# Start addresses modulo 512 bytes of TensorE's operands, and row maxima that begin one step later, in a gated attention and MLP kernel

## The chip, the cores and the metric

The kernel runs on one core of one Trainium2 chip. The metric is the device time of one execution in microseconds (us), as a median of several runs. A second number is the span of a profiled execution: the time from its first to its last recorded instruction, a little less than that execution's device time.

## The reference

The input x has 2048 tokens of 448 numbers. A gate, an attention block with 16 heads of 28, and an MLP behind a layer norm are computed from the same x and mixed.

```python
qkv = (x @ wqkv).reshape(B, S, 3, H, Dh)          # 16 heads of 28
scores = einsum("bhqd,bhkd->bhqk", q, k) * Dh**-0.5
a = (softmax(scores) @ v) @ wo
h = gelu(layernorm(x) @ w1 + b1)                  # 448 -> 1792
b = h @ w2 + b2                                   # 1792 -> 448
g = sigmoid((x * gate_w).sum(-1, keepdims=True))
out = g * a + (1 - g) * b
```

Everything is float32.

## The kernel before

**Precision.** Nearly every matrix is split in two, a high part in TensorE's rounded fp32 form and the low rest. A product a·b becomes three matmuls in a row: high·high, high·low, low·high. In the code the parts carry an h or an l at the end of their names (`w2h`, `w2l`, `hh`, `hl`, `qh`, `ql`, `khi`, `klo`, `woh`, `wol`, `oh`, `ol`).

**The two operands of a matmul.** A matmul first loads a block of 128 columns of one matrix into the array (the weight load, PEld in the profile). This text calls it the fixed matrix. Then the rows of the other matrix stream through it, up to 512 columns; this is the moving matrix. `mlp2` keeps 128 columns of `hh` or `hl` fixed and moves a 448-column row of `w2h` or `w2l` (1792 bytes in each partition, that is 3.5 times 512). The output projection keeps a piece of the attention's result fixed and moves `woh` or `wol`, 448 columns too. In the attention's scores a 128-token piece of the keys is fixed and 512 query columns of `qh` or `ql` move.

**Stages, in order of time.**

1. Up to 113.6 us: q, k and v. Lines L220 and L322 are the q and k products (512 columns), L232 the v product (450 columns, of `wvh` and `wvl`). ScalarE rounds, VectorE and GpSimd subtract, SyncE's queue moves data. `v_tile` sends v from three buffers `vt0` to `vt2` in turn (L236).
2. 113.6 to about 467 us: the MLP, in four chunks c of 512 tokens. `mlp1(c, f)` (L613) makes one of 14 column blocks f in 11 matmuls into PSUM bank f % 2; ScalarE applies gelu twice (L616 into `hh[f]`, L617 into a buffer `h`), GpSimd subtracts (L618 into `hl[f]`). `mlp2(c, i)` (L626, L627, L631) makes one of 16 tiles of 128 tokens in 14 x 3 matmuls. In chunk 0 the weights w1 and w2 are also fetched and split (`high_w1`, `low_w1`, `high_w2`, `low_w2`) between the products.
3. 467 us to the end: attention, in steps of five units (later seven). A unit is one head of a group of four with 128 keys and 512 queries: three products (L563) and an exponential on ScalarE (L567); the four heads' units of one piece of keys then go into the sum over values (L830). The output projection (L735 to L737) runs for each query chunk of the last group.

**Row maxima.** The softmax needs the maximum of each query row before the attention. `RowMax.issue` computes extra score products for it (L440), in groups of six during the MLP: four heads sit in different quarters of the array, so four of them run at the same time, then two more. VectorE reduces each pair (L422). `Filler.spread` sets an even rate between a first step and a limit of 482 such products by the end of the MLP; `Filler.run` is called behind the matmuls and issues a group when it is due. In chunk 0 the spread starts at f == `FS`. The keys for it, `khr`, are loaded by GpSimd's queue at f == 1 (L503, four transfers, one for each quarter), behind the subtraction L618 of f = 0.

**Order.** Instructions of each engine are written in program order and executed in that order. Tile pools are stacks of addresses; a pool that opens takes addresses of a closed one, and the first writer of a tile waits for the last users of whatever lay there. In stage 2 `hh` and `hl` lie where `wh`, `wl`, the staging buffers of q and k, `vt0` to `vt2` and the layer norm's small tiles were.

**Addresses modulo 512 bytes, before.** Counted from the built program: the three moving rows of an mlp2 block start at 0, 256, 0 for f up to 10 and at 0, 0, 0 for f above 10, where a row of 448 columns ends 256 further on than it starts. `hh` and `hl` start at 320 (f up to 6), 256 (7 to 10) and 0 (above 10). The projection moves rows that start at 0 or 256, the high and the low one of a head group at the same offset, and keeps matrices fixed at 256 (384 for the last group, each of whose pieces starts 512 further on). `wvh` and `wvl` start at 0, with `xh` and `xl` fixed at 0. `qh`, `ql` and all keys start at 0. Matrices of 512 columns are 2048 bytes long, so a row of them ends at the offset at which it starts.

Of the kernel before, what the change touches and what calls it, by code (L numbers as in the profile page):

```python
# [7 lines left out]
F32 = mybir.dt.float32  # L8
F32R = mybir.dt.float32r
# [6 lines left out]
P = 128  # L16
S = 2048
D = 448
# [4 lines left out]
CH = 512  # L23
# [7 lines left out]
MLP_MAX = 482  # L31
MLP_G = MLP_MAX // 260
MG = 6
FS = 4
WARM = 10
W1, W2 = 0.233, 0.205
SHIFTS = {10: 64, 6: 16}
LQ = 12
STEPS = (2, 5, 7, 8, 9, 10)
LSTEPS = (1, 3, 5, 6, 7, 8)  # L40
# [3 lines left out]
def kernel(ctx: ExitStack, tc: tile.TileContext, xt, wqk, wv, wo, xk, w1, b1, w2, b2,  # L44
# [38 lines left out]
    w1h, w1l, w2h, w2l = {}, {}, {}, {}  # L83
# [73 lines left out]
    with tc.tile_pool(name="qx", bufs=2) as qx, tc.tile_pool(name="qo", bufs=4) as qo, \  # L157
# [24 lines left out]
            nc.scalar.activation(wh[:, m], wt[m], AF.Copy)  # L182
            nc.gpsimd.tensor_sub(wl[:, m], wt[m], wh[:, m].bitcast(F32))

        wvh, wvl = (qw.tile([P, 4, CH], F32R, name=f"wv{x}")[:, :, :450] for x in "hl")
        vt = [qw.tile([P, H, 32], F32, name=f"vt{i}") for i in range(3)]

        xh, xl = {}, {}
# [112 lines left out]
        for what, i in turns:  # L301
# [18 lines left out]
            for k, m, t in ops:  # L320
                w, x = wl if k == "lh" else wh, xl[0] if k == "hl" else xh[0]
# [48 lines left out]
        for n in range(NM, 11 * NC):  # L370
            for what, a in ahead[n]:
                what(*a)
            c, m = divmod(n, 11)
# [124 lines left out]
    def load_khr(g, k=None, queue=nc.sync):  # L498

        sl = slice(0, S) if k is None else slice(k * CH, (k + 1) * CH)  # L500
        for j in range(4):
            r = D + (4 * g + j) * DH
            queue.dma_start(khr[32 * j:32 * j + DH, sl].bitcast(F32), qk[0, r:r + DH, sl])  # L503
# [27 lines left out]
    qs = {}  # L531

    def load_q(n):

        g, c = divmod(n, NC)
        qs[n] = aq.tile([P, CH], F32R, name="qh", bufs=3), aq.tile([P, CH], F32R, name="ql", bufs=3)
        for i in range(2):
            for j in range(4):
                r = (4 * g + j) * DH
                nc.sync.dma_start(qs[n][i][32 * j:32 * j + DH].bitcast(F32), qk[i, r:r + DH, c * CH:(c + 1) * CH])  # L540
# [52 lines left out]
    mw2 = ml.enter_context(tc.tile_pool(name="mw2", bufs=1, reuse_waits="tile"))  # L593
    mh = ml.enter_context(tc.tile_pool(name="mh", bufs=1, reuse_waits="tile"))
    for f in range(NF):
        w2h[f], w2l[f] = (mw2.tile([P, CH if f > 10 else D], F32R, name=f"w2{x}{f}")[:, :D] for x in "hl")
    hh, hl = {}, {}
    more = [mh.tile([P, CH], F32, name=f"more{i}") for i in range(2)]
    for f in reversed(range(NF)):
        if f in SHIFTS:  # L600
            mh.tile([P, SHIFTS[f]], F32, name=f"shift{f}")
        hh[f] = mh.tile([P, CH], F32R, name=f"hh{f}")
        hl[f] = mh.tile([P, CH], F32R, name=f"hl{f}")

    def mlp1(c, f):

        ps = bank[:, f % 2]
        ops = []
        for t in range(3):
            ops += [(w1h[f][:, t], yh[:, t]), (w1h[f][:, t], yl[:, t]), (w1l[f][:, t], yh[:, t])]  # L610
        ops += [(w1h[f][:, 3], yh[:, 3]), (w1l[f][:, 3], yh[:, 3])]
        for i, (a, b) in enumerate(ops):
            nc.tensor.matmul(ps, a, b, start=(i == 0), stop=(i == len(ops) - 1))  # L613
            filler.run(W1 if c else 0.65 * W1)
        h = mh.tile([P, CH], F32, name="h", bufs=2)
        nc.scalar.activation(hh[f], ps, AF.Gelu_apprx_tanh, bias=b1s[:, f:f + 1])  # L616
        nc.scalar.activation(h, ps, AF.Gelu_apprx_tanh, bias=b1s[:, f:f + 1])  # L617
        nc.gpsimd.tensor_sub(hl[f], h, hh[f].bitcast(F32))  # L618
# [21 lines left out]
    with texts:  # L640
# [12 lines left out]
        for c in range(NC):  # L653
            for f in range(NF):
                if c == 0:
# [9 lines left out]
                    if f == 1:  # L665
                        load_khr(0, queue=nc.gpsimd)
                    if f == FS:
                        filler.spread(nc.sync, MLP_MAX, 11 * W1 * (0.65 * (NF - FS) + 3 * NF) + W2 * (3 * NF * (NT - 1) - 24))
                mlp1(c, f)
# [7 lines left out]
            if c == NC - 1:  # L677
                m0.close()
                aq = ctx.enter_context(tc.tile_pool(name="aq", bufs=1, side="right", reuse_waits="tile"))

                first = {3: aq.tile([P, S], F32, name="klo", bufs=2), 2: aq.tile([P, NT, P], F32, name="vg", bufs=2)}

                def early(n, p):
                    t = first[n] if n == 3 else first[n].rearrange("p a b -> p (a b)")
                    return t[:, :n * CH].rearrange("p (n c) -> p n c", c=CH)

                nc.scalar.activation(gate, zall, AF.Exp, scale=-1.0)
                load_khi(0)
                load_klo(0)
                load_q(0)  # L690
                load_v(0)
                load_qm(0)
            else:
                ln_load(c + 1)
                ln_fetch(c + 1, 0)
                ln_fetch(c + 1, 1)
# [15 lines left out]
    def sb(name, bufs, side="left"):  # L712
        return ctx.enter_context(tc.tile_pool(name=name, bufs=bufs, reuse_waits="tile", side=side))

    ap = sb("ap", 4)
    aw = sb("aw", 1)
    ao = sb("ao", 2)
    woh = aw.tile([P, NG, D], F32R, name="woh")
    wol = aw.tile([P, NG, D], F32R, name="wol")

    b2b = aw.tile([P, D], F32, name="b2b")
    sel = aw.tile([P, P], F32, name="sel")

    outcome = [[aw.tile([P, S], F32R, name=f"o{x}{g}") for x in "hl"] for g in range(NG - 1)]
    acc = {}

    def project(c, i, oh, ol, po, groups):

        sl = slice(i * P, (i + 1) * P)
        for g in groups:  # L730
            if g < NG - 1:
                h, l = (x[:, c * CH:(c + 1) * CH][:, sl] for x in outcome[g])
            else:
                h, l = oh[:, sl], ol[:, sl]
            nc.tensor.matmul(po, h, woh[:, g], start=(g == 0), stop=False)  # L735
            nc.tensor.matmul(po, h, wol[:, g], start=False, stop=False)  # L736
            nc.tensor.matmul(po, l, woh[:, g], start=False, stop=(g == NG - 1))  # L737

    def gated(c, i, po):
        tt = c * TPC + i  # L740
        a = acc[c][:, i]
        nc.vector.scalar_tensor_tensor(a, po, gate[:, tt:tt + 1], a, op0=OP.mult, op1=OP.add)
        nc.sync.dma_start(out[tt], a)

    def finish(g, c, pv):

        ob = ao.tile([P, CH], F32, name="ob")
        rc = ao.tile([P, CH], F32, name="rc")
        lt = ao.tile([P, CH // 32], F32, name="lt")
        nc.vector.tensor_copy(ob, pv)  # L750
        nc.gpsimd.dma_start(lt, ob[DH:P:32, :])  # L751
        yield True
        nc.vector.reciprocal(lt, lt)
        r = rls[g * NC + c]
        nc.gpsimd.dma_start(r.rearrange("j (a b) -> (j a) b", b=CH // 32), lt)
        for j in range(4):
            nc.gpsimd.dma_start(rc[32 * j:32 * j + 32], r[j].partition_broadcast(32))
        yield True
        if g < NG - 1:
            oh, ol = (x[:, c * CH:(c + 1) * CH] for x in outcome[g])  # L760
        else:
            oh, ol = ao.tile([P, CH], F32R, name="oh", bufs=1), ao.tile([P, CH], F32R, name="ol", bufs=1)
        nc.gpsimd.tensor_mul(ob, ob, rc)
        nc.gpsimd.tensor_copy(oh, ob)
        nc.gpsimd.tensor_sub(ol, ob, oh.bitcast(F32))
        if g < NG - 1:
            return
        yield True
        for i in range(TPC):
            po = bank[:, 6, :D]  # L770
            project(c, i, oh, ol, po, range(NG))
            gated(c, i, po)
            yield True
# [61 lines left out]
    with tc.manual_schedule(engines=ENGINES):  # L835
# [7 lines left out]
        while u < 4 * steps:  # L843
# [4 lines left out]
            while at < units[-1] // 4:  # L848
                at += 1
                n, k = divmod(at, NT)  # L850
                g, c = divmod(n, NC)
# [18 lines left out]
                if k == 2 and n + 1 < NG * NC:  # L870
                    load_q(n + 1)
# [28 lines left out]
            if ended:  # L900
                n = summed // NT - 1
                fin, since, when = finish(n // NC, n % NC, pv), 0, LSTEPS if late else STEPS
                next(fin)
            elif fin is not None and since in when:
                next(fin, None)
# [58 lines left out]
```

## Time and profile before

| | |
|---|---|
| median of 3 runs | 1114.77 us (1114.1 to 1116.31) |
| profiled execution: its own time | 1114.39 us |
| profiled execution: span | 1112.6 us |
| TensorE matmul busy | 1104.5 us (99% of the span) |
| TensorE weight load busy | 675.4 us (61%) |
| VectorE busy | 741.3 us (67%) |
| ScalarE busy | 634.7 us (57%) |
| GpSimd busy | 334.2 us (30%) |

The clock that TensorE was granted is 1.0 throughout. Matmuls overlap in the record: the duration of one is longer than the distance to the next one's start, and the busy share of TensorE cannot show whether it runs at its peak. What one matmul costs is therefore read from starts: the time from the start of the first of a stretch to the start behind the last, divided by their number. A line such as "113.63 14.94 PE L613 MATMUL ... x65" of the timeline gives the start, the time from there to the end of the last, engine, line and count; "[0.66 <-issue]" behind it is idle time before it and what ended it.

### The profile page before, as it was taken

How to read it: one execution, taken by the hardware profiler on the slowest of the kernel's cores; microseconds unless marked ns; L12 is line 12 of the kernel's file. 1: busy time of each engine (PE TensorE's matmuls, PEld its weight loads, DVE VectorE, ACT ScalarE, POOL GpSimd, SP SyncE). 2: the span in 40 equal slices, each digit the busy share in tenths (PEclk: the TensorE clock that was granted, in tenths of full speed). 3: DMA queues.
4: the chain of work that ended last, by engine and by line, in shares of the span. 5: the costliest groups of instructions: out<-in, count | busy, mean ns of one | idle time of the engine just before them, and what ended most of it. 6: DMA issues, size and time to landing. Idle time of an engine off the chain costs nothing.

```text
span 1112.6 us, 19807 instructions
## 1 busy us (share of the span) xinstructions
PE 1104.5 (99%) x8156; PEld 675.4 (61%) x8156; DVE 741.3 (67%) x1030; ACT 634.7 (57%) x660; POOL 334.2 (30%) x354
## 2 busy tenths in 40 slices
PE   9999999999999999999999999999999999999998
PEld 7888777777777767744444444444444444454545
DVE  4553488988988889576676766667667667746103
ACT  5334640331240232287887887877878878847572
POOL 5025664343334331013112221320223024342350
PEclk9999999999999999999999999999999999999999
DMA  7988641011121022162100220012011003002111
GB/s 266 356 275 272 177 123 44 9 47 46 41 56 37 25 63 77 52 159 77 28 20 19 61 75 18 20 28 53 29 56 37 18 20 94 12 26 70 51 36 59
DMA packets 53079, 84.35 MB, mean 76 GB/s; under 512 B 8516, under 2 KB 28500, under 8 KB 52076
## 3 DMA queue, kind: packets, MB, share of 16 engines
q1 hardware_dynamic: 48732, 76.27, 22.0%
q0 software_dynamic: 4256, 6.81, 2.5%
q8 instruction: 64, 1.05, 0.4%
q14 instruction: 27, 0.22, 0.1%
HBM read 56.40 MB, written 26.49 MB: 75 GB/s over the span
## 4 chain that ended last, share of the span: by engine, by line
PE 98%; DVE 1%; ACT 1%; DMA 1%; issue 0%; SPq 0%; ACTq 0%
PE bank L830 22%; PE bank L563 20%; PE bank L440 16%; PE bank L613 13%; PE bank L220 5%; PE bank L631 5%; PE bank L626 4%; PE bank L627 4%; PE bank L232 3%; PE bank L322 1%; PE bank L735 1%; PE bank L736 1%; PE bank L737 1%; DMA raw<-in_xt 1%; ACT khi L567 0%
## 5 line engine op out<-in xcount | busy, mean ns | idle before, releaser
L567 ACT ACTIVATE pt<-bank 128x1536 f32<-128x1536 f32 (+1 forms) x386 | 460.1, 1242 | 121.8 <-PE bank L563 121.8
L420 DVE TENSOR_REDUCE mx<-bank 128x1 f32<-128x512 f32 x618 | 409.6, 687 | 174.3 <-PE bank L440 160.1
L830 PE MATMUL bank<-pt,vg 128*32 128x512 f32 x1942 | 260.4, 602 | 0.0
L422 DVE TENSOR_REDUCE mx<-bank 128x2 f32<-128x1024 f32 x203 | 238.8, 1219 | 29.9 <-PE bank L440 29.6
L440 PE MATMUL bank<-khi,qd 28*128 28x512 f32 x512 | 241.8, 480 | 0.1
L440 PEld LDWEIGHTS bank<-khi,qd 28*128 28x128 f32 x512 | 92.6, 182 | 148.1 <-DVE mx L420 106.0
L563 PE MATMUL bank<-qh,klo 28*128 28x512 f32 x1024 | 174.3, 394 | 0.0
L563 PE MATMUL bank<-qh,khi 29*128 29x512 f32 x768 | 156.5, 481 | 0.8 <-ACT khi L567 0.6
L613 PE MATMUL bank<-y,w1f 128*128 128x512 f32 x616 | 151.9, 398 | 0.0
L613 PEld LDWEIGHTS bank<-y,w1f 128*128 128x128 f32 x616 | 112.7, 188 | 33.1 <-issue 10.9
L563 PE MATMUL bank<-ql,khi 28*128 28x512 f32 x768 | 129.1, 390 | 0.0
L618 POOL TENSOR_TENSOR hl<-h,hh 128x512 fp32r<-128x512 f32 x56 | 72.9, 1301 | 117.6 <-ACT h L617 77.5
L616 ACT ACTIVATE hh<-bank,b1s 128x512 fp32r<-128x512 f32 x56 | 38.6, 689 | 99.0 <-PE bank L613 97.5
L830 PEld LDWEIGHTS bank<-pt,vg 128*32 128x32 f32 x1942 | 44.7, 108 | 78.5 <-issue 78.0
L563 PEld LDWEIGHTS bank<-qh,klo 28*128 28x128 f32 x1024 | 87.5, 185 | 3.5
L637 ACT ACTIVATE h<-bank 128x448 f32<-128x448 f32 x16 | 8.7, 546 | 137.5 <-PE bank L631 103.3
L751 POOL DMA_DIRECT2D lt<-ob x15 | 10.9, 725 | 252.6 <-DVE ob L750 252.6
L631 PE MATMUL bank<-w2h,hl 128*128 128x448 f32 x224 | 84.9, 379 | 0.0
L563 PEld LDWEIGHTS bank<-qh,khi 29*128 29x128 f32 x768 | 60.7, 182 | 39.6 <-ACT pt L567 24.9
L626 PE MATMUL bank<-w2h,hh 128*128 128x448 f32 x224 | 83.2, 371 | 0.0
L627 PE MATMUL bank<-w2l,hh 128*128 128x448 f32 x224 | 81.8, 365 | 0.0
L440 PE MATMUL bank<-khr,qd 28*128 28x512 f32 x512 | 80.4, 467 | 0.9 <-issue 0.7
(135 smaller groups left out, 1296.5 us busy)
## 6 DMA issues: line engine op xcount, KB each, us to landing
qk<-hl SPq DMA_DIRECT2D x28, 512.0 KB
raw<-in_xt SPq DMA_DIRECT2D x16, 256.0 KB
vs<-vt SPq DMA_DIRECT2D x16, 256.0 KB
s<-in_xt SPq DMA_DIRECT2D x16, 256.0 KB
rc<-rls POOLq DMA_DIRECT2D x60, 64.0 KB, 2.2
w1f<-in_xk SPq DMA_DIRECT2D x8, 448.0 KB
gbs<-h SPq DMA_DIRECT2D x16, 224.0 KB
klo<-qk SPq DMA_DIRECT2D x16, 224.0 KB
```

The source lines that it names most:

```text
L220: nc.tensor.matmul(ps, a, b, start=(i == 0), stop=(i == len(ops) - 1))
L420: nc.vector.reduce_max(self.mx[:, c0:c0 + 1], bank[:, b0], axis=AX)
L422: nc.vector.reduce_max(self.mx[:, c0:c1 + 1:c1 - c0], bank[:, b0:b1 + 1], axis=AX)
L440: nc.tensor.matmul(bank[:, b], self.qds[self.n][r, i * P:(i + 1) * P], khi[self.n // NC][r, k * 512:(k + 1) * 512], start=True, stop=True)
L563: nc.tensor.matmul(bank[:, p], a[r, k * P:(k + 1) * P], b[r], start=(i == 0), stop=(i == 2))
L567: nc.scalar.activation(t, bank[:, at[0]:at[-1] + 1], AF.Exp, scale=SCALE)
L613: nc.tensor.matmul(ps, a, b, start=(i == 0), stop=(i == len(ops) - 1))
L618: nc.gpsimd.tensor_sub(hl[f], h, hh[f].bitcast(F32))
L626: nc.tensor.matmul(a, hh[f][:, sl], w2h[f], start=(f == 0), stop=False)
L627: nc.tensor.matmul(a, hh[f][:, sl], w2l[f], start=False, stop=False)
L631: nc.tensor.matmul(a, hl[f][:, sl], w2h[f], start=False, stop=(f == NF - 1))
L830: nc.tensor.matmul(pv[32 * j:32 * j + 32, :], vg[n // NC][:, k, 32 * j:32 * j + 32], probs.pop(4 * step + j), start=(k == 0), stop=(k == N ...
```

## The change

The weights of the second MLP product are packed without gaps, and for odd f the low part lies in front of the high part, so that the moving rows of one f start at 0, 256, 0 and those of the next at 256, 0, 256: each starts where the last one ended, modulo 512. `hh` and `hl` all start at 64. `wol` moves 256 bytes on, so that a high and a low row follow each other in the same way; the attention's results start at 64 (320 for the last group). `wvh` and `wvl` start at 192 (their rows still don't begin where the last ended: 450 columns are 1800 bytes). `qh` starts at 64, with `ql` and the keys at 0 as before. The row maxima's spread starts at f = 5 instead of 4, with the same limit of 482 products.

```diff
-FS = 4
+FS = 5
-SHIFTS = {10: 64, 6: 16}
+LINE = 16
...
-        wvh, wvl = (qw.tile([P, 4, CH], F32R, name=f"wv{x}")[:, :, :450] for x in "hl")
+        wvh, wvl = (qw.tile([P, 4, CH], F32R, name=f"wv{x}")[:, :, 3 * LINE:3 * LINE + 450] for x in "hl")
...
-        qs[n] = aq.tile([P, CH], F32R, name="qh", bufs=3), aq.tile([P, CH], F32R, name="ql", bufs=3)
+        qs[n] = (aq.tile([P, CH + P], F32R, name="qh", bufs=3)[:, LINE:LINE + CH],
+                 aq.tile([P, CH], F32R, name="ql", bufs=3))
...
-        w2h[f], w2l[f] = (mw2.tile([P, CH if f > 10 else D], F32R, name=f"w2{x}{f}")[:, :D] for x in "hl")
+        t = {x: mw2.tile([P, D], F32R, name=f"w2{x}{f}") for x in ("lh" if f % 2 else "hl")}
+        w2h[f], w2l[f] = t["h"], t["l"]
     hh, hl = {}, {}
     more = [mh.tile([P, CH], F32, name=f"more{i}") for i in range(2)]
+    mh.tile([P, LINE], F32, name="shift")
     for f in reversed(range(NF)):
-        if f in SHIFTS:
-            mh.tile([P, SHIFTS[f]], F32, name=f"shift{f}")
         hh[f] = mh.tile([P, CH], F32R, name=f"hh{f}")
         hl[f] = mh.tile([P, CH], F32R, name=f"hl{f}")
...
     woh = aw.tile([P, NG, D], F32R, name="woh")
+    aw.tile([P, 4 * LINE], F32, name="gap")
     wol = aw.tile([P, NG, D], F32R, name="wol")
...
+    aw.tile([P, LINE], F32, name="shift")
     outcome = [[aw.tile([P, S], F32R, name=f"o{x}{g}") for x in "hl"] for g in range(NG - 1)]
...
+        if not (g or c):
+            ao.tile([P, 2 * LINE], F32, name="gap", bufs=1)
```

What else this does to the program, read from the built order of instructions: the number of instructions is the same on every engine, and in the attention their order is the same too. The row maxima still come in 81 groups; the first stands one f later (behind the tenth product of f = 6 instead of f = 5), four instead of five fall into chunk 0's `mlp1`, and the last groups stand where they stood. Since `hh` and `hl` lie 1792 bytes lower, some waits move. ScalarE's table load ahead of the first gelu waited for a VectorE result and the layer norm's DMAs; now a wait for the products of f = 0, and for the DMA of `vt2`, stands ahead of it. The wait for the DMA of the last `vt0` moves from f = 2 to f = 1. On SyncE the second load of the row maxima's queries (four transfers) goes behind two weight loads instead of ahead of them.

## The prediction

> **What bounds the kernel.** I read the page first: busy shares, granted clock, and the chain that ended last.
>
> ```profile
> PE 1104.5 (99%) x8156; PEld 675.4 (61%) x8156; DVE 741.3 (67%) x1030; ACT 634.7 (57%) x660; POOL 334.2 (30%) x354
> ...
> PEclk9999999999999999999999999999999999999999
> ...
> PE 98%; DVE 1%; ACT 1%; DMA 1%; issue 0%; SPq 0%; ACTq 0%
> PE bank L830 22%; PE bank L563 20%; PE bank L440 16%; PE bank L613 13%; PE bank L220 5%; PE bank L631 5%; PE bank L626 4%; PE bank L627 4%; PE bank L232 3%; PE bank L322 1%; PE bank L735 1%; PE bank L736 1%; PE bank L737 1%; DMA raw<-in_xt 1%; ACT khi L567 0%
> ```
>
> TensorE is on the path for 98% of the span, at full clock. So a nanosecond saved on a matmul is a nanosecond saved, and the change is about nothing but such nanoseconds. Its parts touch mlp2 (13% of the chain), the projection and v (3% each), the scores (20%). The busy time can't price them; starts can. The chain in order of time has long stretches of one line:
>
> ```profile
> 25.02 8.95 PE bank L232 x44
> 33.96 17.49 PE bank L220 x77
> 87.07 12.52 PE bank L220 x55
> 99.81 5.04 PE bank L220 x22
> ```
>
> L220 moves 512 columns, each row starting where the last ended: 17.49/77 = 227.1 ns, 12.52/55 = 227.6, 5.04/22 = 229.1. L232 moves 450 columns and jumps by 248 bytes at each start: 8.95/44 = 203.4. Then mlp2, in stretches of the timeline with no row maxima between (first and last start of twelve products each, at f = 0 to 4, 9 to 13, and 8 to 12):
>
> ```profile
> 175.29 0.37 PE L626 MATMUL bank<-w2h,hh 128*128 128x448 f32 x1
> ...
> 177.71 0.37 PE L626 MATMUL bank<-w2h,hh 128*128 128x448 f32 x1
> ...
> 250.02 0.36 PE L626 MATMUL bank<-w2h,hh 128*128 128x448 f32 x1
> ...
> 252.45 0.36 PE L626 MATMUL bank<-w2h,hh 128*128 128x448 f32 x1
> ...
> 159.62 0.36 PE L626 MATMUL bank<-w2h,hh 128*128 128x448 f32 x1
> ...
> 162.10 0.37 PE L626 MATMUL bank<-w2h,hh 128*128 128x448 f32 x1
> ```
>
> That is 605, 607.5 and 620 ns for a block of three products, or 201.7, 202.5 and 206.7 each. The first stretch jumps once in three starts; the second mixes both layouts; the third does too, and is the dearest I found. So something other than the column count does cost up to 5 ns, but the layout alone doesn't decide it.
>
> **The second MLP product.** There are 16 x 14 = 224 blocks of three. With no jumps the nearest row is L220's 227.1 ns, less 64 columns. A column costs at most 227.1/512 = 0.444 ns and, by the difference of L220 and L232, at least (227.1 - 203.4)/62 = 0.382. So 448 columns would take 198.7 to 202.7 ns; I take the middle, 200.7, or 602 a block. Against 606, between the two common stretches, that is -4 ns x 224 = -0.90 us. Ends: 198.7 (596 a block) gives -2.2 us; the other end is no gain, and 206.7 everywhere would give +3.1 us.
>
> **The projection.** Its 192 products run at
>
> ```profile
> 1077.11 0.36 PE L735 MATMUL bank<-woh,oh 128*128 128x448 f32 x1
> ...
> 1078.73 0.36 PE L737 MATMUL bank<-woh,ol 128*128 128x448 f32 x1
> ```
>
> 1.62/8 = 202.5 ns. Going to 200.7 gives -0.35 us; ends 198.7 and 206.7, -0.7 and +0.8 us.
>
> **The v product.** 176 products keep their jump; only the distance to the fixed matrix changes. I take nothing; the ends are 227.1 x 450/512 = 199.6 (-0.7 us) and 206.7 (+0.6 us).
>
> **Row maxima one step later.** The first group stalls today, the second doesn't:
>
> ```profile
> 113.63 14.94 PE L613 MATMUL bank<-y,w1f 128*128 128x512 f32 x65
> 128.50 0.50 PE L440 MATMUL bank<-khr,qd 28*128 28x512 f32 x3
> 129.66 0.51 PE L440 MATMUL bank<-khr,qd 28*128 28x512 f32 x3 [0.66 <-issue]
> 130.09 4.83 PE L613 MATMUL bank<-y,w1f 128*128 128x512 f32 x20
> 134.85 0.73 PE L440 MATMUL bank<-khr,qd 28*128 28x512 f32 x6
> 135.51 0.73 PE L613 MATMUL bank<-y,w1f 128*128 128x512 f32 x2
> ```
>
> 130.09 - 128.50 = 1.59 us against 135.51 - 134.85 = 0.66: the fourth quarter's product comes 0.93 us late. What it waits for is its quarter of the keys, sent by GpSimd's queue:
>
> ```profile
> 117.71 1.29 POOL L618 TENSOR_TENSOR hl<-h,hh 128x512 fp32r<-128x512 f32 x1 [5.87 <-ACT h L617]
> 118.94 2.27 POOL L503 DMA_DIRECT2D khr<-qk x4
> ...
> DMA to landing us min/median/max: 6.9/7.6/8.9
> ```
>
> The last of the four is issued at about 120.7 and 8.9 later it is 129.6, where the product starts. One step is 11 x 14.87/65 = 2.52 us, so a start at 131.0 finds the keys there: -0.93 us. The group count is the same, so no group's cost is added.
>
> **The table load.** It is the one wait that the lower addresses put in a bad place:
>
> ```profile
> 114.45 1.28 ACT L616 ACT_TABLE_LOAD   x1
> 116.37 0.69 ACT L616 ACTIVATE hh<-bank,b1s 128x512 fp32r<-128x512 f32 x1 [0.64 <-PE bank L613]
> 116.95 0.68 ACT L617 ACTIVATE h<-bank,b1s 128x512 f32<-128x512 f32 x1
> 118.91 0.69 ACT L616 ACTIVATE hh<-bank,b1s 128x512 fp32r<-128x512 f32 x1 [1.27 <-issue]
> ```
>
> Today it fits in the 1.9 us before the products of f = 0 are done at 116.37. Behind that wait it pushes both gelus by 1.28 us: the second ends at 118.91 instead of 117.63. Queued behind it on ScalarE is f = 1's gelu, which starts at 118.91 anyway. TensorE waits for it too: f = 2 reuses the bank of f = 0 and starts at 113.63 + 22 x 0.2288 = 118.66. That is 0.25 us late, with the hand-over 0.3: +0.30 us (ends 0 and 0.6). GpSimd waits as well: its subtraction ends 1.28 later, and behind it stand the four transfers of the keys. They would land at 130.9, and the first group comes at 131.0 + 0.3 = 131.3. The cover is 0.4 us; without it the stall is back in part, at most by the 0.93 that I booked. SyncE's moved loads of the next queries have the time of some seven groups of row maxima; they cost nothing.
>
> **The scores.** One step of the attention:
>
> ```profile
> 708.84 0.50 PE L440 MATMUL bank<-khi,qd 28*128 28x512 f32 x1
> 708.85 0.51 PE L563 MATMUL bank<-qh,khr 29*128 29x512 f32 x3
> 709.19 0.40 PE L563 MATMUL bank<-qh,klo 28*128 28x512 f32 x3
> 709.42 0.39 PE L563 MATMUL bank<-ql,khr 28*128 28x512 f32 x3
> 709.55 0.50 PE L563 MATMUL bank<-qh,khr 29*128 29x512 f32 x2
> 709.66 0.39 PE L440 MATMUL bank<-khi,qd 28*128 28x512 f32 x1
> 709.89 0.40 PE L563 MATMUL bank<-qh,klo 28*128 28x512 f32 x2
> 710.12 0.49 PE L440 MATMUL bank<-khi,qd 28*128 28x512 f32 x1
> 710.54 1.07 PE L830 MATMUL bank<-pt,vg 128*32 128x512 f32 x8
> 711.54 0.50 PE L440 MATMUL bank<-khi,qd 28*128 28x512 f32 x1
> ```
>
> It takes 2.70 us, some 200 times (1024 units, five at a time, later seven). Today everything in it starts at 0, so nothing jumps. With qh alone at 64 the moving row jumps when qh follows something else or is followed by it: about six times a step, 1200 in all. For that the keys lie 64 bytes from qh, and three rounds a step follow each other at 0.23 us, so that their pace is the stream's and not a weight load's. Neither price is in the trace, since nothing jumps by 64. The spread in mlp2 bounds both: (620 - 605)/3 = 5 ns. So the jumps cost at most 1200 x 5 = +6.0 us, the distance gives at most 3 x 200 x 5 = -3.0 us. The common stretches differ by only 2.5 ns in a block, less than 1 ns a product, which is the nearer row, and at such prices the two cancel: I take nothing.
>
> **The sum.** -0.90 - 0.35 - 0.93 + 0.30 = -1.88 us on the profiled execution's 1114.39, which is 0.4 below the median: 1112.5 us. A measurement of this kernel can tell about 0.2% from no change, 2.2 us; against the median the forecast lies at that bound.
>
> **The rivals.**
>
> *Addresses cost TensorE nothing.* The 605 and 607.5 of two quite different layouts speak for it, the 620 against. Then only the two stalls count: 1114.39 - 0.63 = 1113.8 us. Two pages of the Trainium skill say as much: "SBUF — State Buffer", section "SBUF: two separate sides", gives TensorE ports of its own on which it waits for nobody, and "TensorE: Matmul & The Clock Gate", section "Back-to-back issue gap", gives a distance of the columns at 2.4 GHz plus 2.5 ns, with no term for an address. By that rule 512 and 448 columns take 215.8 and 189.2 ns; the trace has 227.1 and 201.7, so it does not agree in size, and something that the rule lacks is in these 11 to 12 ns.
>
> *The distance pays in the scores.* The three rounds a step gain the full 5 ns while jumps by 64 cost little: 1112.5 - 3.0 = 1109.5 us. For it speaks that the stage is the longest and that keys and queries now start at one offset; against it that L220 does so too and runs no slower for its length than mlp2.
>
> *The jumps of qh make it slower.* Each of 1200 new jumps costs the 5 ns of the worst stretch: 1112.5 + 6.0 = 1118.5 us. It decides from 4.5/1200 = 3.8 ns a jump, where 1117.0 is passed. For it speaks that L232, which jumps at every start, takes 203.4 where L220's pace would give 199.6; against it that several jumps fall on rounds which wait for a weight load (709.19 after 708.85 is 0.34, not 0.23).
>
> **Chances.** Forecast 0.38, the scores pay 0.26, addresses cost nothing 0.16, slower by jumps 0.20. Some 0.24 of the forecast's case lies beyond the bound, and nearly all of the second: faster 0.49. The rest of the forecast, the third case and a little of the fourth: same 0.32; slower 0.19. The range leaves out about a tenth at each end, the full prices of the two cases in the scores: 1109.3 to 1116.8 us; the forecast's own is 1111.0 to 1114.0.
>
> **What would show it.** In the timeline: no idle time before the fourth product of the first group of row maxima; the table load at 116.4 and the products of f = 2 some 0.3 us late; blocks of mlp2 at 602 ns at every f, the projection near 201 ns, v still at 203. In the attention, the distance of two steps: 2.70 us if I am right, 2.685 if the distance pays, 2.73 if the jumps do harm. Mlp2 blocks that stay at 606 would refute the main term, steps off by over 10 ns the zero for the scores.

## The result: 0.3% slower, and where the time went

The changed kernel takes 1118.41 us (median of 7 runs, 1117.95 to 1119.56); the kernel before, run beside it, 1114.16 us (1113.36 to 1116.31). The ratio is 1.0032, with a 95% interval of 1.0021 to 1.0043. The forecast was 1112.5 us, in a range of 1109.3 to 1116.8: wrong in sign, and the time lies outside the range. The profiled execution of the changed kernel took 1119.22 us, with a span of 1117.4 against 1112.6 before.

The page of the changed kernel, its busy line and its chain that ended last (shares of the span by engine, then by line):

```profile
PE 1108.0 (99%) x8156; PEld 677.4 (61%) x8156; DVE 749.9 (67%) x1030; ACT 634.5 (57%) x660; POOL 333.7 (30%) x354
...
PE 94%; DVE 3%; issue 1%; ACT 1%; DMA 0%; SPq 0%; DVEq 0%; ACTq 0%
PE bank L836 22%; PE bank L564 20%; PE bank L440 15%; PE bank L615 11%; PE bank L220 5%; PE bank L633 4%; PE bank L628 4%; PE bank L629 4%; PE bank L232 3%; DVE mx L422 2%; PE bank L322 1%; PE bank L739 1%; PE bank L740 1%; PE bank L741 1%;
```

VectorE now holds 3% of the chain, 2% with the reductions of the row maxima (L422). Before, it held 1% and no single line of it was listed. The stages say where. Each goes from the first start of one line's products in the timeline to the first start of the next one's; the attention is taken from its first product behind the last one of mlp2, because five of its units already stand inside mlp2's last tile:

| stage | before, us | after, us | difference |
|---|---|---|---|
| up to the first product of mlp1 | 113.63 | 113.94 | +0.31 |
| mlp1, chunk 0 | 40.27 | 38.99 | -1.28 |
| **mlp2, chunk 0** | **43.04** | **49.56** | **+6.52** |
| mlp1 and mlp2, chunks 1 to 3 | 270.47 | 270.41 | -0.06 |
| attention up to the first product of the projection | 512.94 | 512.44 | -0.50 |
| the rest, to the end of the span | 132.26 | 132.07 | -0.19 |

The sum is +4.8, the difference of the spans. Nearly all the loss lies in one stage, in which no weight was added, and of products only one group of six row maxima. In the timeline of the changed kernel (start, time from there to the end of the last, engine, line, count, idle time before and what ended it), the first tile of that stage reads:

```profile
155.86 0.73 PE L440 MATMUL bank<-khr,qd 28*128 28x512 f32 x6
...
159.46 0.37 PE L629 MATMUL bank<-w2l,hh 128*128 128x448 f32 x1
160.51 0.50 PE L440 MATMUL bank<-khr,qd 28*128 28x512 f32 x2 [0.69 <-DVE mx L422]
161.64 0.50 PE L440 MATMUL bank<-khr,qd 28*128 28x512 f32 x2 [0.63 <-DVE mx L422]
162.77 0.79 PE L440 MATMUL bank<-khr,qd 28*128 28x512 f32 x2 [0.63 <-DVE mx L422]
163.50 0.74 PE L633 MATMUL bank<-w2h,hl 128*128 128x448 f32 x1
164.03 0.57 PE L628 MATMUL bank<-w2h,hh 128*128 128x448 f32 x1
...
168.89 0.57 PE L629 MATMUL bank<-w2l,hh 128*128 128x448 f32 x1
...
170.36 0.37 PE L628 MATMUL bank<-w2h,hh 128*128 128x448 f32 x1
...
172.79 0.37 PE L628 MATMUL bank<-w2h,hh 128*128 128x448 f32 x1
```

A group of six row-maxima products goes through in one piece at 155.86. The next one comes out two by two, each pair waiting for a reduction: from 159.46 to 163.50, 4.0 us, where such a step takes about 1.0 (L629 to L633 with a group between them). After it thirteen distances of mlp2's products take 168.89 - 164.03 = 4.86 us, 374 ns each; from 170.36 to 172.79 twelve take 2.43, 202.5 ns each. The windows view of the same stretch (length, then busy time and count of PE, PEld, DVE, ACT and POOL, then the granted clock of TensorE, the DMA engines' share and GB/s):

```profile
159.00:161.00 2.00, 1.31 (x7) 0.60 (x5) 2.00 (x3) 0.00 (x0) 0.00 (x0) 1.00 0.81 185
161.00:163.00 2.00, 0.74 (x6) 0.41 (x4) 2.00 (x3) 0.00 (x0) 0.33 (x1) 0.90 0.63 219
163.00:165.00 2.00, 2.00 (x6) 1.43 (x7) 2.00 (x3) 0.00 (x0) 1.92 (x2) 0.50 0.00 0
```

VectorE is busy without a break, TensorE for 1.31 and 0.74 of 2 us, and from about 162.6 to 169.4 us TensorE was granted half its clock. So the stage pays three times: some 3 us of waiting, some 2.7 us of products at half clock, and 0.8 us for one group that the later start moved into this stage from mlp1 of chunk 0 (which is why mlp1 became shorter by more than its stall).

Why VectorE was behind stands 35 us earlier, in chunk 0 of mlp1. Rows of the timeline of the changed kernel (engines ACT, DVE, POOL):

```profile
116.69 1.28 ACT L618 ACT_TABLE_LOAD   x1 [1.95 <-PE bank L615]
...
126.42 7.01 DVE L118 TENSOR_TENSOR w2l<-lnr,w2h 128x448 fp32r<-128x448 f32 x1 [3.38 <-ACT w2h L115]
...
159.25 6.87 DVE L422 TENSOR_REDUCE mx<-bank 128x2 f32<-128x1024 f32 x6
...
126.68 1.29 POOL L620 TENSOR_TENSOR hl<-h,hh 128x512 fp32r<-128x512 f32 x1
127.93 1.28 POOL L108 TENSOR_TENSOR w1f<-s,w1f 128x512 fp32r<-128x512 f32 x1
...
131.68 1.27 POOL L620 TENSOR_TENSOR hl<-h,hh 128x512 fp32r<-128x512 f32 x1
```

And of the kernel before:

```profile
125.61 1.55 DVE L118 TENSOR_TENSOR w2l<-lnr,w2h 128x448 fp32r<-128x448 f32 x1 [2.59 <-ACT w2h L115]
...
125.38 1.30 POOL L618 TENSOR_TENSOR hl<-h,hh 128x512 fp32r<-128x512 f32 x1
126.63 1.69 POOL L108 TENSOR_TENSOR w1f<-s,w1f 128x512 fp32r<-128x512 f32 x1
```

The same subtraction of w2's low part takes 7.01 us instead of 1.55. Before, VectorE gets in behind the GpSimd operation that runs when it is issued (125.38 + 1.30), and GpSimd's next one waits for it (1.69 instead of 1.28). After, GpSimd is 1.6 us later (its subtraction of f = 0 starts at 119.32 instead of 117.71; 1.3 us of that is the table load, the rest the later start of mlp1). VectorE's subtraction is issued at 126.42. Five GpSimd operations, the first at 126.68 and the last at 131.68, follow each other without a gap to 132.95, and VectorE's ends only behind the last of them, at 133.43. The Trainium skill, page "SBUF — State Buffer", section "SBUF: two separate sides", says that a VectorE operation with two inputs in SBUF and a GpSimd operation that reads SBUF need the same pair of ports, which one of them holds for the whole of its instruction. The trace agrees with that. By the same section of the Trainium skill, whichever starts first gets the pair; it leaves open who is next when both have work waiting. Here VectorE lost five times in a row.

From then on VectorE runs behind. The subtractions of the last weights end at 159.3, which is 6.4 us into mlp2; with the same start of the row maxima and the early table load (a kernel below) they end 3.5 us into it. Only then come six reductions, of the group of 155.86 and of the next, one behind the other (6.87 us). TensorE waits for them.

### The profile page after: what moved, and what is told of

Same layout as the page of the kernel before. It is cut to its first block, busy times and chain, and to the rows that moved or that the text cites. A ratio compares the mean times of both kernels' runs of the same rounds, so it can differ in the third digit from the quotient of the medians.

```text
span 1117.4 us, 19808 instructions
## 1 busy us (share of the span) xinstructions
PE 1108.0 (99%) x8156; PEld 677.4 (61%) x8156; DVE 749.9 (67%) x1030; ACT 634.5 (57%) x660; POOL 333.7 (30%) x354
## 4 chain that ended last, share of the span: by engine, by line
PE 94%; DVE 3%; issue 1%; ACT 1%; DMA 0%; SPq 0%; DVEq 0%; ACTq 0%
PE bank L836 22%; PE bank L564 20%; PE bank L440 15%; PE bank L615 11%; PE bank L220 5%; PE bank L633 4%; PE bank L628 4%; PE bank L629 4%; PE bank L232 3%; DVE mx L422 2%; PE bank L322 1%; PE bank L739 1%; PE bank L740 1%; PE bank L741 1%; DVE w2l L118 1%
## 5 line engine op out<-in xcount | busy, mean ns | idle before, releaser
L422 DVE TENSOR_REDUCE mx<-bank 128x2 f32<-128x1024 f32 x203 | 238.8, 1219 | 27.9 <-PE bank L440 27.5
L440 PE MATMUL bank<-khi,qd 28*128 28x512 f32 x512 | 241.7, 479 | 0.1
L440 PEld LDWEIGHTS bank<-khi,qd 28*128 28x128 f32 x512 | 92.4, 181 | 148.4 <-DVE mx L420 105.3
L633 PE MATMUL bank<-w2h,hl 128*128 128x448 f32 x224 | 86.1, 384 | 0.0
L440 PE MATMUL bank<-khr,qd 28*128 28x512 f32 x512 | 81.2, 468 | 2.1 <-DVE mx L422 2.1
L629 PE MATMUL bank<-w2l,hh 128*128 128x448 f32 x224 | 82.6, 369 | 0.0
```

Source lines behind the costliest of these rows:

```text
L422: nc.vector.reduce_max(self.mx[:, c0:c1 + 1:c1 - c0], bank[:, b0:b1 + 1], axis=AX)
L440: nc.tensor.matmul(bank[:, b], self.qds[self.n][r, i * P:(i + 1) * P], khi[self.n // NC][r, k * 512:(k + 1) * 512], start=True, stop=True)
L629: nc.tensor.matmul(a, hh[f][:, sl], w2l[f], start=False, stop=False)
L633: nc.tensor.matmul(a, hl[f][:, sl], w2h[f], start=False, stop=(f == NF - 1))
```

## The experiments

Three theories were set against each other. T1: the later start of the row maxima does it alone. T2: the table load, which now waits for the products of f = 0, puts GpSimd late; VectorE's subtraction is locked out, VectorE falls behind, and the groups that the later start puts into the first tile of mlp2 run into it. T3: the new addresses do it (the jumps of `qh`). T2 stands here in the form that it took after the first run; before that run it said that VectorE's lateness alone would do it, whatever the start. Stage lengths below are taken as in the table above.

### Changed kernel, row maxima from f = 4 again

```diff
-FS = 5
+FS = 4
```

> The changed kernel with the row maxima starting at f = 4 again; all its addresses stay. Theory 1 (the late start alone: it puts two groups of row maxima into the first tile of mlp2 while VectorE still splits w2): no group waits for VectorE in that tile, the clock stays at 1.0, and what is left is the addresses: 1114.5 us, between 1113.5 and 1115.5. Theory 2 (the displaced wait before the table load lets GpSimd run without a gap, VectorE's subtraction for f = 1 takes 7 us instead of 1.6, and VectorE never catches up): that subtraction still takes about 7 us and a group still waits by more than 1 us: 1117 to 1118.5 us. Theory 3 (the jumps of qh and the other addresses cost it): 1118 us, with the attention longer than before; the attention's span in the changed kernel, 0.7 us shorter than before, speaks against it already.

Measured: 1115.34 us, ratio to the kernel before 1.0002 (0.9991 to 1.0014). The loss is gone, though the new addresses and the late table load (117.24 us) are there. But VectorE's subtraction is still locked out:

```profile
126.94 5.79 DVE L118 TENSOR_TENSOR w2l<-lnr,w2h 128x448 fp32r<-128x448 f32 x1 [3.33 <-ACT w2h L115]
...
158.69 1.58 DVE L118 TENSOR_TENSOR w2l<-s,w2h 128x448 fp32r<-128x448 f32 x1
160.72 3.49 DVE L422 TENSOR_REDUCE mx<-bank 128x2 f32<-128x1024 f32 x3 [0.46 <-PE bank L440]
...
153.08 0.73 PE L440 MATMUL bank<-khr,qd 28*128 28x512 f32 x6
160.19 0.73 PE L440 MATMUL bank<-khr,qd 28*128 28x512 f32 x6
```

With this start no group falls between 153.08 and 160.19, and VectorE has caught up by then. So T3, which had 1118 us for this kernel, is out. T2 as it was first written, 1117 to 1118.5 us, failed too, and the time was that of T1: the late VectorE alone makes no group wait in mlp2. It isn't free: mlp1 of chunk 0 takes 40.94 us here and 40.11 with the early table load (a run below), mainly because TensorE waits for the late gelu at f = 2, and the second and third group for VectorE (their steps take 0.84 and 1.09 us, and 0.69 and 0.66 there).

### Kernel before, row maxima from f = 5

```diff
-FS = 4
+FS = 5
```

> The kernel before with the row maxima starting at f = 5; no address changes. Theory 1: the group at f = 9 of the first tile of mlp2 waits for VectorE for 2 to 3 us, the clock falls to 0.5 for about 7 us, and the time is 1117.5 to 1119 us. Theory 2: VectorE's subtraction for f = 1 takes under 2 us, no group waits for more than 0.5 us, the clock stays at 1.0, and the time is that of before less the first group's stall of 0.93 us: 1113.2 us. Theory 3: 1113.2 us as well.

Measured: 1113.84 us, ratio 0.9990 (0.9980 to 0.9999). Mlp1 of chunk 0 takes 38.48 us instead of 40.27, mlp2 43.83 instead of 43.04 (the moved group). T1 is out: the later start alone is a small gain.

### Changed kernel, early table load

1536 bytes more under the hidden tiles put them off the buffer `vt2` that made the table load wait; modulo 512 every address stays.

```diff
-    mh.tile([P, LINE], F32, name="shift")
+    mh.tile([P, LINE + 384], F32, name="shift")
```

> The changed kernel with 1536 bytes more ahead of hh and hl, three times 512, so that every address is the same modulo 512 but hh of f = 0 no longer lies on vt2: the table load stands ahead of the wait for the products again, as before the change. Row maxima still start at f = 5. Theory 1: the stall and the half clock stay; only the table load's 0.3 us goes: 1118 us. Theory 2: the subtraction for f = 1 takes under 2 us, the group at f = 9 waits by less than 0.5 us, the clock stays at 1.0: 1112.5 to 1113.5 us. Theory 3: 1118 us without stall.

Measured: 1113.43 us, ratio 0.9986 (0.9977 to 0.9996). In its timeline the load is early, the subtraction short, and the groups of the first tile go through:

```profile
115.45 1.28 ACT L618 ACT_TABLE_LOAD   x1
...
126.59 1.54 DVE L118 TENSOR_TENSOR w2l<-lnr,w2h 128x448 fp32r<-128x448 f32 x1 [2.58 <-ACT w2h L115]
...
156.06 0.73 PE L440 MATMUL bank<-khr,qd 28*128 28x512 f32 x6
159.96 0.73 PE L440 MATMUL bank<-khr,qd 28*128 28x512 f32 x6
```

### Early table load, row maxima from f = 4

```diff
-FS = 5
+FS = 4
...
-    mh.tile([P, LINE], F32, name="shift")
+    mh.tile([P, LINE + 384], F32, name="shift")
```

> The fourth corner: the table load early (the hidden tiles three times 512 bytes higher, as in the kernel with the wider shift), row maxima from f = 4, all other addresses as in the changed kernel. T2 (the loss needs both the late table load and the later start): 1114.0 to 1115.0 us, no half clock, VectorE's subtraction of f = 1 at 1.5 us, the first group's stall of before back. T1 (the later start alone): as the kernel of before, 1114.2. T3 (addresses): 1116 or more.

Measured: 1114.31 us, ratio 0.9996 (0.9987 to 1.0006), the subtraction at 1.54 us, mlp1 of chunk 0 at 40.11. That fills the square:

| | row maxima from f = 4 | from f = 5 |
|---|---|---|
| table load early | 0.9996 (new addresses); 1 (before) | 0.9986 (new addresses); 0.9990 (before's) |
| table load late | 1.0002 (new addresses) | **1.0032** (the change); 1.0048 (before's, the next run) |

### Kernel before, made to wait

Every address of the kernel before modulo 512, row maxima from f = 5, and one staging tile moved from below the hidden tiles to above, so that `hh0` comes to lie on `vt2`.

```diff
-FS = 4
+FS = 5
...
-    more = [mh.tile([P, CH], F32, name=f"more{i}") for i in range(2)]
+    more = [mh.tile([P, CH], F32, name="more0")]
...
         hl[f] = mh.tile([P, CH], F32R, name=f"hl{f}")
+    more.append(mh.tile([P, CH], F32, name="more1"))
```

> The kernel of before, every address as it was modulo 512 bytes, with row maxima from f = 5 and one of the two staging tiles allocated after the hidden tiles instead of before them, so that hh0 lies 2048 bytes lower and the table load waits behind the products of f = 0. T2: the loss is back without any of the new addresses: table load near 116.6, VectorE's subtraction of f = 1 at 5 to 7 us, groups of row maxima in the first tile of the second MLP product that wait for VectorE, a stretch at half clock, 1117.5 to 1119.5 us. T3 (addresses): 1113.8, as the kernel of before with row maxima from f = 5.

Measured: 1119.87 us, ratio 1.0048 (1.0033 to 1.0063). The time is a little above the expected range, the rows are those expected:

```profile
116.94 1.28 ACT L617 ACT_TABLE_LOAD   x1 [1.98 <-PE bank L614]
...
126.63 7.06 DVE L118 TENSOR_TENSOR w2l<-lnr,w2h 128x448 fp32r<-128x448 f32 x1 [3.33 <-ACT w2h L115]
...
160.82 0.50 PE L440 MATMUL bank<-khr,qd 28*128 28x512 f32 x2 [0.74 <-DVE mx L422]
```

The whole loss, without one of the new addresses modulo 512: T2 holds, and T3 falls again.

### Filling the wait

Twelve products that nothing uses, of 2.4 us, ahead of the block f = 9 of the first tile.

```diff
         for f in range(NF):
+            for _ in range(12 if c + i == 0 and f == 9 else 0):
+                nc.tensor.matmul(bank[:, 1, :D], hh[0][:, sl], w2h[0], start=True, stop=True)
             nc.tensor.matmul(a, hh[f][:, sl], w2h[f], start=(f == 0), stop=False)
```

> The changed kernel with twelve products of 448 columns into a free bank, just before the block of the second MLP product's first tile in which the row maxima wait for VectorE (f = 9); they are not used. They take 12 x 0.2 = 2.4 us, the time that TensorE waits there today, so the wait is filled and not removed. If TensorE's half clock after that wait is what makes the loss larger than the wait (T2), it goes, the products after it run at 0.2 us again, and the time is 1118.4 - 2.9 = 1115.5 us, though the kernel does more. If the half clock is only a companion, or has another cause than the idle time, the time is 1118.4 or up to 2.4 more.

Measured: 1116.99 us, ratio 1.0018 (1.0009 to 1.0028), 1.5 us more than expected but less than the change itself, with twelve products more:

```profile
160.18 2.59 PE L629 MATMUL bank<-w2h,hh 128*128 128x448 f32 x12
...
163.10 1.09 PE L440 MATMUL bank<-khr,qd 28*128 28x512 f32 x6
...
164.44 0.36 PE L630 MATMUL bank<-w2h,hh 128*128 128x448 f32 x1
...
166.86 0.36 PE L630 MATMUL bank<-w2h,hh 128*128 128x448 f32 x1
```

The twelve distances after the group take 2.42 us, full clock, and the stage 46.62 us instead of 49.56: the 2.9 us expected. The half clock came from TensorE's idle time and is some 2.7 to 2.9 us of the loss; the wait for VectorE is as much again (46.62 against the 43.83 us of the kernels without it). Why the whole gained only 1.4 us was not settled; in the traced execution mlp1 begins 1.0 us later than in the changed kernel's (114.91 against 113.94), though no instruction ahead of it differs.

### Fewer groups at the start

```diff
-            rows = not last and (c * TPC + i < NT - 2 or f < 10) and (c + i > 0 or f > 3)
+            rows = not last and (c * TPC + i < NT - 2 or f < 10) and (c + i > 0 or f > 6)
```

> The changed kernel, but in the first tile of mlp2 the row maxima may stand only behind f = 6 instead of f = 3. Nothing before that tile changes, so the subtraction for f = 1 still takes about 7 us. It prices the stall itself: if the wait for VectorE and the half clock behind it are the loss (theories 1 and 2), the first group of that tile stands at f = 7, VectorE is done with w2 soon after, and 4 to 6 us come back: 1112.5 to 1114.5 us, clock 1.0. If the loss is elsewhere (theory 3), 1118 us.

Measured: 1120.73 us, ratio 1.0055 (1.0040 to 1.0070): a miss. The early stall is nearly gone (from the first product of mlp1 to the first of the projection it takes 864.2 us; the change 871.4, the kernel with the early table load 864.9). But only 467 products of row maxima then lie ahead of the attention instead of 475, and the eight that lack are caught up near the end (L440, one at a time, each waiting for its reduction):

```profile
1036.30 0.58 PE L440 MATMUL bank<-khi,qd 28*128 28x512 f32 x1 [0.78 <-DVE mx L420]
...
1037.00:1040.00 3.00, 2.08 (x14) 1.61 (x15) 1.10 (x3) 0.02 (x1) 0.00 (x0) 0.50 0.03 5
```

The clock halves there too, and the part from the projection on is 9 us longer (136.8 instead of 127.8). The experiment moved the collision, and showed the same pair of costs at a second place.

### v's weights back at 0

The kernel with the early table load, and:

```diff
-        wvh, wvl = (qw.tile([P, 4, CH], F32R, name=f"wv{x}")[:, :, 3 * LINE:3 * LINE + 450] for x in "hl")
+        wvh, wvl = (qw.tile([P, 4, CH], F32R, name=f"wv{x}")[:, :, :450] for x in "hl")
```

> The changed kernel with the early table load (wider shift) and the v product's fixed matrices at their old offset 0 again. 44 products of v go back from 9.09 to 8.95 us, four times: 1113.4 - 0.56 = 1112.9 us. If the 0.14 us comes from something else than the offset of the fixed matrices, they stay at 9.09 and the time at 1113.4.

Measured: 1113.41 us, ratio 0.9995 (0.9986 to 1.0005). In the chain, 44 products of v take 8.95 us again; the first line is of this kernel, the second of the changed one:

```profile
25.34 8.95 PE bank L232 x44
```

```profile
24.80 9.09 PE bank L232 x44
```

So the offset of 192 costs 0.14 us four times, 0.56 in all: 206.6 ns for a product instead of 203.4. The median cannot tell that much; the rows can. (The expectation calls `wvh` and `wvl` the fixed matrices of the v product; they are the moving ones.)

### The queries at 64 alone

```diff
-FS = 4
+FS = 5
...
-        qs[n] = aq.tile([P, CH], F32R, name="qh", bufs=3), aq.tile([P, CH], F32R, name="ql", bufs=3)
+        qs[n] = (aq.tile([P, CH + P], F32R, name="qh", bufs=3)[:, 16:16 + CH],
+                 aq.tile([P, CH], F32R, name="ql", bufs=3))
```

> The kernel of before with row maxima from f = 5 and qh alone at 64 bytes. If qh's offset is what shortens the attention, the stretch from its first product to the first product of the projection goes from 512.9 to 512.3-512.5 us and the time from 1113.8 to 1113.4, which the time alone can hardly tell; the projection part stays at 127.96. If other tiles of that stage do it, the stretch stays at 512.9. If the jumps cost what the rival of the prediction says, it is 515 or more.

Measured: 1113.18 us, ratio 0.9991 (0.9982 to 1.0000). First products of the attention and of the projection, in its timeline, and below it in that of the kernel before with row maxima from f = 5:

```profile
468.66 0.73 PE L564 MATMUL bank<-qh,khi 29*128 29x512 f32 x4
...
981.15 0.47 PE L736 MATMUL bank<-woh,oh 128*128 128x448 f32 x1
```

```profile
466.94 0.73 PE L563 MATMUL bank<-qh,khi 29*128 29x512 f32 x4
...
979.87 0.47 PE L735 MATMUL bank<-woh,oh 128*128 128x448 f32 x1
```

512.49 against 512.93 us. The three kernels with `qh` at 0 have 512.92 to 512.97, all with `qh` at 64 have 512.31 to 512.60. The query offset gains 0.4 to 0.5 us, some 2 ns a step of the attention.

### The keys on SyncE's queue

The changed kernel, late table load and all, with the four transfers that hold GpSimd for 2.27 us moved away from it.

```diff
-                        load_khr(0, queue=nc.gpsimd)
+                        load_khr(0)
```

> The changed kernel with the four transfers of the keys issued on SyncE's queue instead of GpSimd's; the table load stays late. GpSimd is then 2.27 us less behind when VectorE's subtraction of f = 1 comes. T2 (the subtraction is locked out because GpSimd runs late): table load near 116.7 as before, but that subtraction at 1.5 to 2 us, no group of row maxima that waits for VectorE in the second MLP product, no half clock, 1113.0 to 1114.5 us. If the late table load does its harm by another way than GpSimd's lateness (ScalarE's gelus, the products of f = 2), the loss stays: 1117 or more.

Measured: 1121.64 us, ratio 1.0066 (1.0051 to 1.0080): the mechanism as expected, the time not.

```profile
126.92 1.35 DVE L118 TENSOR_TENSOR w2l<-lnr,w2h 128x448 fp32r<-128x448 f32 x1 [4.04 <-ACT w2h L115]
...
128.63 0.63 ACT L105 ACTIVATE w1f<-lnr 128x512 fp32r<-128x512 f32 x1 [1.74 <-DMA lnr<-in_w]
...
1108.66 0.36 PE L741 MATMUL bank<-woh,ol 128*128 128x448 f32 x1
```

With GpSimd less late the subtraction takes 1.35 us, no group waits, the clock stays full, mlp2 of chunk 0 takes 43.81 us: it is GpSimd's lateness by which the table load does its harm. The transfers now stand ahead of weight fetches on SyncE's queue, for one of which ScalarE waits 1.74 us. That is a second change in this run. But the subtraction got in where the GpSimd operation of 126.50 ended, while GpSimd's next one (127.75, 1.68 us) already waited for it, so before ScalarE's wait could leave GpSimd without work. The last product starts at 1108.66, earlier than in the changed kernel (1113.14). But the span ends 9.8 us after that start, instead of 4.3 us: a drain, one of GpSimd's closing instructions, takes 10.97 us in the trace, 1.41 in the changed kernel and 1.74 at most in every kernel that has the keys on GpSimd's queue. Why is open.

### All that paid, together

Early table load, v at 0, `qh` at 64, row maxima from f = 5 and the keys on SyncE's queue: the kernel with v at 0, above, and the line just shown.

> The parts that paid, together: row maxima from f = 5, table load early (wider shift), v's fixed matrices at 0, queries at 64, and the keys on SyncE's queue, so that GpSimd is never behind. Expected 1112.5 to 1113.4 us: the 1113.4 of the kernel with early table load, less up to 0.9 if GpSimd's earlier run lets a group's wait go that is left. Nothing of it can be slower than the kernel of before unless the keys, now ahead of four fetches of weights on SyncE's queue, make those late (then 1115 or more).

Measured: 1122.57 us, ratio 1.0069 (1.0056 to 1.0082): a miss, by the exception that the expectation names. ScalarE waits 3.83 us for the delayed weights, TensorE loses the clock once in mlp1 of chunk 0 (42.82 us instead of 38.5), and the closing drain takes 10.97 us here as well.

> The same kernel as with the early table load and v's fixed matrices at 0, in more rounds, to see whether what is left of the change beats the kernel of before: by its stages it saves the first group's wait (0.9 us) and some 0.4 in the attention, so 1.3 us or a ratio of 0.9988; if only noise was seen in its single parts, 1.0000.

This is the same kernel without the last line, that is, the keys on GpSimd's queue. Measured: 1112.92 us, ratio 0.9981 (0.9971 to 0.9991). In its first run the same kernel had 0.9995 (0.9986 to 1.0005), so it beats the kernel before by 0.1 to 0.2%, and the change by some 0.4 to 0.5%.

## Why the prediction was wrong

**Where it failed.** In two sentences that are one. "The group count is the same, so no group's cost is added" put the moved group at nothing: it priced the row maxima by their own products, and not by when VectorE can take them. And under "The table load" GpSimd's 1.28 us were followed to the keys, which are behind GpSimd on a queue, and not to VectorE, which shares ports with it. Both parts were priced by themselves, where the loss is in the two together: +5.7 us in mlp2 of chunk 0 (49.56 against 43.83 in the kernels without the wait), half of it waiting, half half clock. None of the four cases of the prediction had such a loss. VectorE's 67% looked like slack. From 126 to 160 us, where it subtracts weights and reduces, it is busy for 28.76 of 34 us in the kernel before; 5.2 us are left, and the long subtraction takes 5.5 us more. In the changed kernel it is busy for 33.58. The windows of the kernel before and, below it, of the changed one:

```profile
126.00:160.00 34.00, 33.34 (x163) 24.99 (x162) 28.76 (x27) 20.45 (x37) 25.02 (x19) 1.00 0.48 136
```

```profile
126.00:160.00 34.00, 33.82 (x163) 25.76 (x162) 33.58 (x24) 21.26 (x38) 26.41 (x20) 1.00 0.47 129
```

How little is left was to be read from the trace of before, where in the first tile of mlp2 the last subtraction ends 0.46 us ahead of the reductions of a group:

```profile
157.16 1.57 DVE L118 TENSOR_TENSOR w2l<-s,w2h 128x448 fp32r<-128x448 f32 x1
159.19 3.49 DVE L422 TENSOR_REDUCE mx<-bank 128x2 f32<-128x1024 f32 x3 [0.46 <-PE bank L440]
```

**The row maxima's own stall, -0.93.** Right. The first group now goes through:

```profile
113.94 5.17 PE L615 MATMUL bank<-y,w1f 128*128 128x512 f32 x22
119.30 12.57 PE L615 MATMUL bank<-y,w1f 128*128 128x512 f32 x54 [0.19 <-ACT h L619]
131.81 0.73 PE L440 MATMUL bank<-khr,qd 28*128 28x512 f32 x6
132.47 4.85 PE L615 MATMUL bank<-y,w1f 128*128 128x512 f32 x20
```

132.47 - 131.81 is 0.66 us, the length of a group that does not wait; and the keys were there in time, as worked out. SyncE's moved loads cost nothing either: TensorE waits for no transfer in the MLP.

**The table load, +0.30 on TensorE.** Right at that place: 119.30 is 0.33 later than 113.94 + 22 x 0.2288. Mlp1 of chunk 0 as a whole is 0.5 longer than with the early load (38.99 against 38.50).

**The second MLP product, -0.90.** Mis-sized, and the reason given for it is wrong. Four blocks from 170.36 to 172.79 are 607.5 ns each, not 602. The mean of all blocks with nothing between them (some 164 of the 224 in each trace, from starts) shows what happened:

| blocks | `hh`, `hl` start at, old layout | four kernels with the old layout, ns | ten with the new one, ns |
|---|---|---|---|
| f = 0 to 6 | 320 | 606.3 | 606.8 |
| f = 7 to 10 | 256 | 610.0 | 606.4 |
| f = 11 to 13 | 0 | 609.8 | 606.4 |

Up to f = 6 the old layout jumps once in each block and is as fast as the new one, so that jump costs nothing. From f = 7 the old layout has blocks of up to 621 ns, among them the prediction's stretch of 620, and the new one has none above 617. That makes 1 to 2 ns a block over all f, or -0.2 to -0.4 us. Chunks 1 to 3 say the same between kernels with row maxima from f = 5: 270.65 to 270.72 us with the old layout, 270.30 to 270.48 with the new one. The moving rows are the same for f = 7 to 10 as for f up to 6, and only the start of the fixed matrices differs, so it looks like a matter of their distance; but no run moves `hh` and `hl` alone. Of the rivals, "Addresses cost TensorE nothing" came nearest to this part.

**The projection, -0.35.** Mis-sized: the part from the projection to the last product is 127.80 us instead of 127.96, and it is 127.8 in every kernel with the new layout but the one that caught up there, 128.0 to 128.1 in those without. Some -0.2. The row of eight products could not show that: 1 ns a product.

**The v product, 0.** Mis-sized: +0.56, the upper end that was given (206.6 ns, 206.7 forecast as the bound). So addresses do count, here, in mlp2 and in the scores, a few ns at a time. Which rule they follow stays open: in v a jump at every start was there before and after, and it is the larger distance, 192 instead of 0, that is dearer.

**The scores, 0.** The ends of -3.0 and +6.0 were far too wide; it is -0.4 to -0.5. "The jumps of qh make it slower" had the time, 1118.5, by luck and nothing else: the new offset gains.

Without the late load the parts as measured give -0.93 + 0.56 - 0.45 - 0.2 - 0.3 = -1.3 us; the kernel with the early table load has 1113.43 us against 1114.52 of the kernel before beside it, -1.1.

## What to carry to other kernels

A later instruction is not paid where it stands only: follow the delay along every engine that shares a queue, a buffer or a port with the one that is late, until it meets slack. An engine's share of the whole says nothing of its slack in a stage; list its operations there, and see how long ahead of the next consumer the last one ends. Price a small effect by the mean over all like rows of a trace, set out by what differs between them, and not by three stretches. When addresses are changed, read the waits that the new overlaps make before reading the gains, and where the waits of a TensorE at full clock grow towards 2 us in a few us (1.8 to 2.4 in 3.4 were enough here), count the clock with them.

## What the runs showed of the hardware that was not expected

**Half clock after a short wait.** TensorE idle for 1.8 of some 3.4 us was followed by half the clock for 6.8 us (162.6 to 169.4), though the waits were over at 162.8. Filled with products, the same stretch kept its clock. The kernel before made to wait ran at half clock for 3.4 us (1.9 us idle ahead of it), the one with fewer groups for 10.2 (2.2 us), and the one with all that paid for 3.4 (2.4 us). Up to 0.6 us of idle time in 3.4, in the middle of a kernel, cost no clock in any run. Where the limit lies stays open: at the start, 1.0 and 1.3 us were followed by half the clock in two traces and 1.0 to 1.25 in six others were not, and near the end 1.7 to 1.8 were not in three. The Trainium skill, page "TensorE: Matmul & The Clock Gate", section "What's actually happening", gives a free-running window of 3413 ns and half the clock after an idle one. The trace agrees with the length: 3.4, 6.8 and 10.2 us are one, two and three windows. But the windows ahead of these drops were only half idle, or up to 70%.

**VectorE can be shut out for several operations of GpSimd.** 5.8 to 7.1 us in the five kernels in which the table load and the keys' transfers both made GpSimd late, 1.35 to 1.55 us in the nine others, though GpSimd's operations follow each other there too. In the five the subtraction is issued 0.95 to 1.00 us into a GpSimd operation of 1.29, in the nine 0.22 to 0.41 us into one. That alone doesn't decide it: subtractions of other weights that were issued 0.94 us into one took 0.85 us. What decides who gets in was not found.

**The drain of GpSimd.** 10.97 us at the end of the two kernels that issue four transfers fewer on its queue, 1.4 to 1.7 in the rest.
